# Windowed attention and a gated spatial unit on one core: every matmul operand as two float16 pieces with fixed scales

## The chip, the cores and the metric

The kernel runs on one core of one Trainium2 chip. The metric is the device time of one execution in microseconds (us); the time before is the median of three runs. One further execution was recorded by the hardware profiler, and all views below are of that one.

The engines of a core are TensorE (PE; its weight loads are listed as PEld), VectorE (DVE), ScalarE (ACT), GpSimd (POOL) and SyncE (SP), which here only issues DMAs. PE writes to PSUM. Each engine works through its instructions in the order in which the program gives them and waits on semaphores for the others.

## The reference

```python
# q, k, v: (4, 8, 768, 64) float32; window 128, 4 sink keys
scores = np.matmul(q, k.transpose(0, 1, 3, 2)) / np.sqrt(D)
keep = is_sink | in_window             # columns 0..3, or 0 <= row - column < 128
a = softmax(np.where(keep, scores, -1e9))          # (sum + 1e-9) below
x = np.matmul(a, v) -> (4, 768, 512)               # heads side by side
h = np.maximum(x @ w_in, 0.0)          # w_in (512, 1024) float64
u, v = h[..., :512], h[..., 512:]
v_n = (v - mean(v)) / np.sqrt(var(v) + 1e-06)
v_s = einsum('ts,bsd->btd', w_spatial, v_n) + b_spatial[None, :, None]
out = ((u * v_s) @ w_out).astype(np.float32)       # w_out (512, 512) float64
```

The inputs are normal draws: q and k have a spread of 0.58, v of 0.1, w_in and w_out of 0.044, w_spatial of 0.00083; b_spatial is about 1.

## The kernel before

Four batches (b), six tiles of 128 rows each (t), two halves of four heads (hf). An attention step (b, t, hf) is a block of score products (`scores`, PE L1027 or L1033, into four PSUM banks `sc`), a mask and row minimum on DVE (L1038), an exponential on ACT (L1043), a split of the weights into two float16 pieces `p high` and `p low` (`weights`), a DMA transpose (L1090), and the product with v (`attend`, L1122 to L1130). When both halves are there, `divide` (L1145 to L1150) makes x, which is split and transposed into `xT`. Then come, for each tile, the product `ps_v` with the second half of w_in, ReLU, normalisation and a split into `vn`; for each pair of tiles (c0) four products `ps_u` with the first half of w_in (d = 0..3, ring `u`), four products `ps_s` of w_spatial with all six `vn` of the batch, gate and product with u (`g`), a split into `g2`, and two products `ps_o` with w_out, whose result ACT copies and SP stores.

A split product is three matmuls: high by high, high by low, low by high (`three`, L758; `scores`, L1033; `product` in `attend`). The pieces are float16 for p, v, x, w_in, vn and w_spatial. They are fp32r (a 4-byte format; the profile writes f32) for q, k, g and w_out: `qp`, `kring`, `ksink`, `g2` and `wout`. Batch 0 has its scores in whole fp32 (L1027), and its first two tiles also the product with v (L1072 transposes, L1139), from the raw loads.

Where a float16 piece is made from v, w_in or w_spatial, it is multiplied by a power of two found at run time. For v of a batch: ACT sums |v| over each of six tiles (L908, `junk`), `all_max` takes the maximum on DVE and PE (L775 to L789: three DVE instructions, two small matmuls), `power_of_two_scale` makes the scale and its inverse (L226, L229). For w_spatial the same (L862). For each half of w_in the clamp in the decoding of float64 (`decode`, L811 on DVE) also gives the maximum, and `scale_from_high_word` makes the scale (L236 to L245). Every high piece (`high`, L726, scale read from a tile) and low piece (`low_scaled`, L747, DVE) of these, the division of the first two tiles (L1146), the ReLUs (L1189, L1237) and the gate (L1258) use such a scale. The window and sink count are compared with the values built in (`Scalars.compare`); a flag decides at the end whether a general path runs in addition.

The order of all work is computed when the kernel is built. `Plan.add` gives each piece a rank, one or more engines with a cost each, what it reads and what it writes; several engines mean that the planner picks one (`ENGINES`: `q low`, `k low`, `p low`, `vn low`, `g low` and the product with u may go to DVE or POOL; `low_scaled` is for DVE alone). Buffers come from rings of fixed size (`UB` 5 for u, `G2B` 6 for g2, `QKB` 2 for the raw q and k), most of them handed out in the order of the ranks. `PASSES` is a list of seeds with which the planner improves its order. The planner's order is then fixed, on each engine and on SP's queue of DMAs.

Of the kernel before, what the change touches and what calls it, by code (L numbers as in the profile page):

```python
# [6 lines left out]
F32 = mybir.dt.float32  # L7
# [3 lines left out]
I32 = mybir.dt.int32  # L11
# [19 lines left out]
TOP_LOW = bits_as_f32(0x39000000)  # L31
# [27 lines left out]
def f64_to_f32(nc, raw, w, tmp, top=None):  # L59

    words = raw.rearrange("p (n two) -> p n two", two=2)
    lo, hi = words[:, :, 0], words[:, :, 1]
    c = w.bitcast(I32)
    nc.scalar.activation(w, hi.bitcast(F32), AF.Abs)
    nc.scalar.activation(tmp, lo.bitcast(U32), AF.Copy, scale=2.0 ** -29)
    if top is None:
        nc.gpsimd.tensor_scalar(w, w, EXP_LOW, EXP_HIGH, op0=ALU.max, op1=ALU.min)
    else:  # L70
        nc.vector.tensor_scalar(w, w, EXP_LOW, None, op0=ALU.max, op1=ALU.max, accum_out=top)
# [147 lines left out]
SUM_SCALE, SUM_FLOOR = 2.0 ** -12, 2.0 ** -112  # L219


def power_of_two_scale(nc, pool, r, name):


    scale = pool.tile([P, 1], F32, name=name + "_scale")
    nc.vector.tensor_scalar(scale.bitcast(I32), r.bitcast(I32), 0x7F800000, 0x7F800000,  # L226
                            op0=ALU.bitwise_xor, op1=ALU.bitwise_and)
    inv = pool.tile([P, 1], F32, name=name + "_inv")
    nc.vector.reciprocal(inv, scale)  # L229
    return scale, inv  # L230


def scale_from_high_word(nc, pool, top, name):

    t = pool.tile([P, 1], F32, name=name + "_top")
    nc.vector.tensor_scalar(t, top, TOP_LOW, EXP_HIGH, op0=ALU.max, op1=ALU.min)  # L236
    n = pool.tile([P, 1], I32, name=name + "_not")
    nc.vector.tensor_scalar(n, t.bitcast(I32), 0x7FFFFFFF, 0x47F00000, op0=ALU.bitwise_xor, op1=ALU.bitwise_and)
    e = pool.tile([P, 1], I32, name=name + "_exp")
    nc.vector.tensor_scalar(e, n, 0x07FFFFFF, 3, op0=ALU.bitwise_and, op1=ALU.logical_shift_left)  # L240
    nc.vector.scalar_tensor_tensor(out=e, in0=n, scalar=0x40000000, in1=e, op0=ALU.bitwise_and, op1=ALU.bitwise_or)
    scale = pool.tile([P, 1], F32, name=name + "_scale")
    nc.vector.tensor_scalar(scale, e.bitcast(F32), 2.0 ** 12, None, op0=ALU.mult)
    inv = pool.tile([P, 1], F32, name=name + "_inv")
    nc.vector.reciprocal(inv, scale)  # L245
    return scale, inv
# [19 lines left out]
UB, VNB, G2B, XTB, P16B, PTB, QKB, QPB, PEB, VB, VRB = 5, 12, 6, 2, 2, 2, 2, 2, 2, 3, 6  # L266
# [30 lines left out]
SCALARS_AT = 27.0  # L297
COLD_TIMES, DMA_START, DMA_LAND = 2.0, 1.7, 1.5
SPELL, ENOUGH = 3.41333, 3030.0
PORT = 0.7  # L300
AHEAD, AHEAD_MOST = 0.05, 0.6
PASSES = ((1000003, 322, 354, 3), (1000006, 123, 212, 1), (1000007, 281, 383, 3), (1000008, 0, 58, 3), (1000009, 0, 11, 3), (1000014, 0, 421, 4), (1000021, 444, 0, 3), (1000329, 316, 0, 3), (1000653, 170, 138, 4), (1000927, 0, 637, 3), (1000987, 377, 68, 2), (1001045, 0, 205, 2), (1001102, 38, 0, 3), (1001131, 528, 106, 3), (1001348, 1242, 212, 4), (1001349, 404, 7, 5), (1001385, 407, 0, 4), (1001398, 113, 172, 3), (1001455, 0, 14, 2), (11000127, 339, 0, 2), (11000189, 0, 74, 3), (11000203, 522, 72, 4), (11000255, 35, 330, 2), (11000353, 0, 145, 2), (11000354, 0, 200, 2), (11000417, 37, 93, 3), (11000494, 926, 48, 2), (11000511, 687, 0, 2), (13001225, 236, 18, 2), (22000675, 339, 205, 5), (22000684, 0, 46, 2), (22000739, 49, 0, 2), (22001001, 265, 0, 2), (37000818, 27, 109, 3), (51001115, 185, 0, 3), (55001266, 648, 0, 4), (73000498, 853, 0, 3),)
# [268 lines left out]
def begin(nc, pool):  # L571
# [7 lines left out]
    st.wout = pool.tile([P, 2, KC, DM], F32R, name="wout")  # L579
# [39 lines left out]
def fast_path(tc, st, scalars, qk, v, v0, vs, w_in, w_sp, b_sp, w_out, out):  # L619
# [7 lines left out]
    with (  # L627
# [14 lines left out]
        kring = const.tile([P, 2, 4, HP, SEG], F32R, name="kring")  # L642
        ksink = const.tile([P, 2, HP, NS], F32R, name="ksink")
# [24 lines left out]
        def next_p16(name):  # L668
# [4 lines left out]
            "dec": ("u", sb([P, 1024], I32, "u", UB)), "junk": ("vr", sb([P, 1024], BF16, "vr", VB)),  # L673
            "u": ("u", sb([P, KC, TC], F32, "u", UB)), "wraw": ("u", sb([P, 1024], F32, "u", UB)),
# [6 lines left out]
            "qp": ("qp", sb([P, 2, HP, P], F32R, "qp", QPB)),  # L681
# [6 lines left out]
            "g": ("g", sb([P, TC], F32, "g", 2)),  # L688
            "g2": ("g2", sb([P, 2, TC], F32R, "g2", G2B)),
# [6 lines left out]
                 "p16": P16B, "pT": PTB, "x": 1, "x16": 2, "xT": XTB, "g": 2, "g2": G2B,  # L696
# [20 lines left out]
        def high(rank, kind, n, views, reads, writes, scale=None):  # L717

            def f(e):
                o, x = views()  # L720
                sc = scale() if scale else None
# [12 lines left out]
            plan.add(rank, ENGINES[kind], costs(kind, n, pointer=scale is not None), f, reads, writes, shared=True)  # L734
# [28 lines left out]
        vals = {}  # L763

        def begin_sums(name, n):
            m = small.tile([P, n + 1], F32, tag="mxs", name="mxs", bufs=1)
            nc.gpsimd.memset(m[:, n:], SUM_FLOOR)
            vals["mx", name] = m

        def all_max(rank, name, cols):  # L770


            def a(e):
                m = vals["m", name] = small.tile([P, 1], BF16, tag="allmax", name="allmax_m")
# [5 lines left out]
            def c(e):  # L780
                m = vals["1", name] = small.tile([1, 1], BF16, tag="allmax1", name="allmax_1")
                nc.vector.tensor_reduce(out=m, in_=tl("ps_row", name)[:1, :P], axis=AX.X, op=ALU.max)

            def d(e):
                nc.tensor.matmul(tl("ps_col", name)[:, :1], st.ones, vals["1", name], start=True, stop=True)

            def f(e):
                r = vals["r", name] = small.tile([P, 1], F32, tag="allmax2", name="allmax_r")
# [7 lines left out]
        def scalar(rank, name, f, t=0.3):  # L796
            plan.add(rank, "d", t, lambda e: f(), [("r", name)], [("scale", name)])


        def decode(rank, src, i, c, f0, top=None):  # L800
# [6 lines left out]
            def clamp(e):  # L807
                if top is None:
                    eng[e].tensor_scalar(w(), w(), EXP_LOW, EXP_HIGH, op0=ALU.max, op1=ALU.min)
                else:  # L810
                    nc.vector.tensor_scalar(w(), w(), EXP_LOW, None, op0=ALU.max, op1=ALU.max, accum_out=top())  # L811
# [578 lines left out]
```

## Time and profile before

| | before |
|---|---|
| median of three runs (lowest, highest) | 434.05 us (432.85, 434.43) |
| profiled execution | 431.45 us |
| its span, first to last instruction | 429.7 us |
| PE / PEld / DVE / ACT / POOL busy in the span | 402.0 / 310.7 / 333.8 / 280.8 / 199.5 us |
| moved by DMA | 64.57 MB |

The span is what the profile shows; 1.75 us of the profiled execution lie outside it. Busy times count an instruction from its start to its end. Matmuls overlap in the pipeline, so the length of one (some 0.27 us for 256 columns) is not its price: that is the distance from the start of one to the start of the next, or the length of a group in the chain of waits divided by its count. Idle time of an engine that is not the bottleneck costs nothing.

### The profile page before, as it was taken

What the parts mean: (1) busy time and instruction counts of PE and PEld (TensorE: products, weight loads), DVE (VectorE), ACT (ScalarE), POOL (GpSimd) and SP (SyncE); (2) the same over time, 40 slices, a digit from 0 to 9 for tenths busy, and PEclk for the clock granted to TensorE, in tenths of its full rate; (3) what the DMA queues carried; (4) which work ended last, traced back from release to release, by engine and by line L of the source; (5) the groups of instructions that cost most, each with busy time, mean ns of one, the idle gap of its engine ahead of it and who ended that gap; (6) DMA issues with size and microseconds to landing.
All of it is one profiled execution on the core that took longest, in us unless ns stands there. A gap on an engine that the chain in (4) does not pass through costs nothing.

```text
span 429.7 us, 9834 instructions
## 1 busy us (share of the span) xinstructions
PE 402.0 (94%) x3646; PEld 310.7 (72%) x3646; DVE 333.8 (78%) x924; ACT 280.8 (65%) x600; POOL 199.5 (46%) x232
## 2 busy tenths in 40 slices
PE   2779888799999999999999999999999999999994
PEld 1558356577887687778768777678777887788883
DVE  2999999998899999769989987577996786336340
ACT  3999778978986888655687675578565754231211
POOL 4425458773995746548435476306552451100000
PEclk9995689999999999999999999999999999999998
DMA  7998699982259899964764899455954355200102
GB/s 227 384 374 240 176 171 210 214 191 63 75 108 251 203 216 199 211 137 64 185 146 132 218 186 163 109 124 90 142 132 105 76 127 129 51 24 2 50 25 80
DMA packets 136039, 64.57 MB, mean 150 GB/s; under 512 B 118192, under 2 KB 122032, under 8 KB 135984
## 3 DMA queue, kind: packets, MB, share of 16 engines
q1 hardware_dynamic: 135984, 63.88, 63.3%
q8 instruction: 30, 0.49, 0.6%
q14 instruction: 25, 0.20, 0.2%
HBM read 28.73 MB, written 6.29 MB: 82 GB/s over the span
## 4 chain that ended last, share of the span: by engine, by line
PE 73%; DVE 14%; ACT 6%; issue 3%; DMA 2%; SPq 0%; POOL 0%; DVEq 0%; ACTq 0%
PE ps_s L758 20%; PE ps_o L758 15%; PE ps_u L758 12%; PE ps_v L758 12%; PE sc L1033 7%; DVE pexp L1038 2%; PE av L1128 2%; PE av L1129 2%; PE av L1130 2%; ACT pexp L1043 1%; DMA dec<-w_in 1%; DVE w L821 1%; DVE p L740 1%; DVE wsp L747 1%; DVE vring L747 1%
## 5 line engine op out<-in xcount | busy, mean ns | idle before, releaser
L758 PE MATMUL ps_s<-wsp,vn 128*128 128x256 f16 x864 | 99.0, 273 | 0.0
L1043 ACT ACTIVATE pexp<-pexp,nm 128x260 f32<-128x260 f32 (+1 forms) x192 | 82.4, 484 | 24.0 <-DVE nm L1038 22.2
L758 PEld LDWEIGHTS <-vn 128*128 128x128 f16 x864 | 82.8, 98 | 11.7 <-issue 0.8
L758 PE MATMUL ps_o<-wout,g 128*128 128x512 f32 x288 | 72.3, 402 | 0.1
L758 PE MATMUL ps_v<-win,xT 128*128 128x512 f16 x288 | 67.6, 385 | 2.6 <-ACT u L1237 2.6
L758 PE MATMUL ps_u<-xT,win 128*128 128x256 f16 x576 | 68.0, 273 | 1.2 <-ACT vr L1189 1.1
L758 PEld LDWEIGHTS <-win 128*128 128x128 f16 x576 | 55.1, 98 | 11.1 <-issue 1.8
L758 PEld LDWEIGHTS ps_o<-wout,g 128*128 128x128 f32 x288 | 52.7, 188 | 12.5 <-ACT ob L1284 0.3
L740 DVE TENSOR_TENSOR p<-pexp,p 128x16 f16<-128x16 f32 (+2 forms) x65 | 56.2, 881 | 4.5 <-ACT p L724 3.9
L758 PEld LDWEIGHTS <-xT 128*128 128x128 f16 x288 | 27.2, 99 | 34.8 <-issue 5.0
L1205 POOL TENSOR_TENSOR rs<-rs,mhalf 128x1 f32<-128x1 f32 x24 | 17.1, 714 | 55.2 <-DVE rs L1199 55.2
L724 ACT CAST p<-pexp 128x32 f16<-128x32 f32 (+2 forms) x69 | 41.8, 627 | 1.1 <-DMA pT<-p 0.6
L740 POOL TENSOR_TENSOR x<-x,x 128x512 f16<-128x512 f32 x24 | 31.6, 1316 | 21.3 <-ACT x L724 20.9
L1258 DVE SCALAR_TENSOR_TENSOR g<-ps_s,isc,b_bc 128x256 f32<-128x256 f32 x48 | 23.0, 480 | 21.1 <-PE ps_s L758 20.0
L724 ACT CAST g<-g 128x256 fp32r<-128x256 f32 x35 | 14.1, 404 | 35.1 <-DVE g L1262 25.6
L1128 PE MATMUL av<-vring,pT 128*128 128x65 f16 x328 | 35.4, 195 | 1.5 <-DMA pT<-p 1.5
L1033 PE MATMUL sc<-kring,qp 64*128 64x260 f32 (+1 forms) x432 | 36.2, 297 | 0.5 <-DVE nm L1038 0.5
L1033 PEld LDWEIGHTS sc<-kring,qp 64*128 64x128 f32 x432 | 28.6, 186 | 9.5 <-issue 6.5
L1130 PE MATMUL av<-vring,pT 128*128 128x65 f16 x328 | 35.3, 195 | 0.0
L1129 PE MATMUL av<-vring,pT 128*128 128x65 f16 x328 | 35.3, 195 | 0.0
L1128 PEld LDWEIGHTS <-pT 128*128 128x128 f16 x328 | 30.8, 99 | 2.7 <-DMA pT<-p 1.7
L1237 ACT ACTIVATE u<-ps_u,icu 128x256 f32<-128x256 f32 x48 | 22.6, 470 | 13.7 <-PE ps_u L758 13.2
(142 smaller groups left out, 741.0 us busy)
## 6 DMA issues: line engine op xcount, KB each, us to landing
qkraw<-qk_t SPq DMA_DIRECT2D x18, 512.0 KB, 4.5
out<-ob SPq DMA_DIRECT2D x24, 256.0 KB, 2.5
vraw<-v_s SPq DMA_DIRECT2D x22, 256.0 KB, 4.2
dec<-w_in SPq DMA_DIRECT2D x8, 512.0 KB, 6.7
dec<-w_out SPq DMA_DIRECT2D x4, 512.0 KB, 6.6
wsp<-qk_t SPq DMA_DIRECT2D x6, 256.0 KB, 6.3
qkraw<-qk_t SPq DMA_DIRECT2D x6, 256.0 KB, 4.8
pT<-p SPq DMA_TRANSPOSE x88, 2.9
```

The source lines that it names most:

```text
L724: nc.scalar.copy(o, x)
L740: eng[e].tensor_tensor(out=o, in0=x, in1=hi, op=ALU.subtract)
L747: nc.vector.scalar_tensor_tensor(out=o, in0=x, scalar=scale(), in1=hi, op0=ALU.mult, op1=ALU.subtract)
L758: nc.tensor.matmul(o, a, m, start=(i == 0), stop=(i == n - 1))
L1033: nc.tensor.matmul(o, qp[rows, qi, hp, :], keys(kring[:, ki], rows), start=(m == 0), stop=(m == 2))
L1043: nc.scalar.activation(po, po, AF.Exp, bias=nm()[:, h2 + q:h2 + q + 1], scale=-1.0)
L1128: nc.tensor.matmul(o[:, h], ph, vh, start=(t < 2 and j == 0), stop=False)
L1129: nc.tensor.matmul(o[:, h], ph, vl, start=False, stop=False)
L1130: nc.tensor.matmul(o[:, h], pl, vh, start=False, stop=(j == nb - 1 and (t < 2 or h == HH - 1)))
L1205: nc.gpsimd.tensor_tensor(out=vals["rs", i], in0=vals["rs", i], in1=mhalf, op=ALU.pow)
L1237: plan.add(r + WHEN["u relu"], "a", 0.36, lambda e: nc.scalar.activation(tl("u", (b, c0))[:, d, :], tl("ps_u", i)[:, :TC], AF.Relu, scale= ...
L1258: nc.vector.scalar_tensor_tensor(out=g(), in0=tl("ps_s", i)[:, :TC], scalar=vals["s", "sp"][1], in1=b_bc[:, t0:t0 + TC], op0=ALU.mult, op1 ...
```

## The change

The scales become constants (16 for q and k, 128 for v, w_in, w_out and for u, 16384 for w_spatial), and with them q, k, g and w_out become pairs of float16 too. So `begin_sums`, `scalar`, `v_scale`, `scale_half`, `power_of_two_scale` and `scale_from_high_word` go; `high` and `low_scaled` take a number. `q low` and `k low` change from `low` (DVE or POOL) to `low_scaled` (DVE), and so does the low piece of w_out (POOL before).

In place of the scales there are range checks at the end of the work: ACT sums |x| of v, of q and k, of w_in and w_out pieces, and of the rows of w_spatial, which are loaded once more (`measure`); the ReLU of u gives its sum as well; `checks` joins them into the flag that decides on the general path. For the inputs above each sum lies well inside its limits. The rank of the new pieces is late (`CHECKS_AT` 56; two steps after the tile's for q and k, four for v).

The ring of u grows from 5 to 7 buffers, that of g2 from 6 to 12 (of half the size). Some costs in the planner are new, and `PASSES` has other seeds, so the whole order is computed anew.

```diff
-UB, VNB, G2B, XTB, P16B, PTB, QKB, QPB, PEB, VB, VRB = 5, 12, 6, 2, 2, 2, 2, 2, 2, 3, 6
+UB, VNB, G2B, XTB, P16B, PTB, QKB, QPB, PEB, VB, VRB = 7, 12, 12, 2, 2, 2, 2, 2, 2, 3, 6
...
-    st.wout = pool.tile([P, 2, KC, DM], F32R, name="wout")
+    st.wout = pool.tile([P, 2, KC, DM], F16, name="wout")
...
-        kring = const.tile([P, 2, 4, HP, SEG], F32R, name="kring")
-        ksink = const.tile([P, 2, HP, NS], F32R, name="ksink")
+        kring = const.tile([P, 2, 4, HP, SEG], F16, name="kring")
+        ksink = const.tile([P, 2, HP, NS], F16, name="ksink")
...
-            "qp": ("qp", sb([P, 2, HP, P], F32R, "qp", QPB)),
+            "qp": ("qp", sb([P, 2, HP, P], F16, "qp", QPB)),
...
-            "g2": ("g2", sb([P, 2, TC], F32R, "g2", G2B)),
+            "g2": ("g2", sb([P, 2, TC], F16, "g2", G2B)),
...
+        def measure(rank, kind, i, n, x, reads, scale):
+            def f(e):
...
+                nc.scalar.activation(o, a, AF.Abs, scale=scale, accum_out=sums[:, first[kind] + i:first[kind] + i + 1])
+            plan.add(rank, "a", 0.22 + n / 1200, f, reads, [("sum", kind, i)])
...
             def clamp(e):
-                if top is None:
-                    eng[e].tensor_scalar(w(), w(), EXP_LOW, EXP_HIGH, op0=ALU.max, op1=ALU.min)
-                else:
-                    nc.vector.tensor_scalar(w(), w(), EXP_LOW, None, op0=ALU.max, op1=ALU.max, accum_out=top())
+                eng[e].tensor_scalar(w(), w(), EXP_LOW, EXP_HIGH, op0=ALU.max, op1=ALU.min)
...
-            all_max(r, name, lambda: mx)
-            scalar(r, name, lambda: vals.__setitem__(
-                ("s", name), scale_from_high_word(nc, scal, vals["r", name], f"win{half}")), 1.0)
...
+            for k in range(2):
+                measure(CHECKS_AT, "win", 2 * half + k, 1024, lambda k=k: win[:, 0, 2 * k:2 * k + 2, f0:f0 + 512],
+                        [("win", half)], 1.0 / F16_RANGE)
...
+                load(CHECKS_AT, "wrow", c, lambda c=c: w_rows[c * P:(c + 1) * P, :], 384, lambda t: t[:, :S])
+                measure(CHECKS_AT, "wsp", c, S, lambda c=c: tl("wrow", c)[:, :S], [("wrow", c)], SP_SCALE / F16_RANGE)
...
-                plan.add(r0 + gap * c, "a", 0.52, lambda e, c=c, i=i: nc.scalar.copy(wout[:, 0, c, :], tl("w32", i)),
-                         [("w32", i)], [("wout", c, 0)])
-                low(r0 + gap * c, "w_out low", 512, lambda c=c, i=i: (wout[:, 1, c, :], tl("w32", i), wout[:, 0, c, :]),
-                    [("w32", i), ("wout", c, 0)], [("wout", c, 1)])
+                high(r0 + gap * c, "w_in high", 512, lambda c=c, i=i: (wout[:, 0, c, :], tl("w32", i)),
+                     [("w32", i)], [("wout", c, 0)], OUT_SCALE)
+                low_scaled(r0 + gap * c, 512, lambda c=c, i=i: (wout[:, 1, c, :], tl("w32", i), wout[:, 0, c, :]), OUT_SCALE,
+                           [("w32", i), ("wout", c, 0)], [("wout", c, 1)])
...
+        def checks():
...
+            plan.add(CHECKS_AT, "d", 0.2, bound, [("sum", "wsp"), ("b_col", 0)], [("mx", "gate")])
+            all_max(CHECKS_AT, "gate", lambda: vals["mx", "gate"])
...
+            plan.add(CHECKS_AT, "d", 0.5, early, [("sum", k) for k in ("v", "win", "wout", "wsp", "qk")], [("most", 0)])
+            plan.add(CHECKS_AT, "d", 0.4, late, [("sum", "u"), ("r", "gate"), ("most", 0)], [("marks", 0)])
+            plan.add(CHECKS_AT, "PE", 0.06, count, [("marks", 0)], [("ps_row", "marks")], columns=26)
+            plan.add(CHECKS_AT, "d", 0.6, decide, [("ps_row", "marks"), ("flag", 0)], [("decision", 0)])
...
+            measure(r + 2, "qk", (b - WHOLE) * NT + t, 1024, lambda: raw().rearrange("p c h s -> p (c h s)"), [("qkraw", i)], Q_SCALE / F16_RANGE)
-            low(r, "q low", 512, lambda: (qp()[:, 1], raw()[:, 0], qp()[:, 0]), [("qkraw", i), ("qp", i, 0)], [("qp", i, 1)])
+            low_scaled(r, 512, lambda: (qp()[:, 1], raw()[:, 0], qp()[:, 0]), Q_SCALE, [("qkraw", i), ("qp", i, 0)], [("qp", i, 1)])
...
-            plan.add(r + WHEN["div"], "d", 1.05, divide, [("av", (b, t))] + ([("scale", ("v", b))] if whole_av(b, t) else []), [("x", (b, t))])
+            plan.add(r + WHEN["div"], "d", 1.05, divide, [("av", (b, t))], [("x", (b, t))])
...
-            plan.add(r + WHEN["u relu"], "a", 0.36, lambda e: nc.scalar.activation(
-                tl("u", (b, c0))[:, d, :], tl("ps_u", i)[:, :TC], AF.Relu, scale=vals["icu", b]),
...
+            plan.add(r + WHEN["u relu"], "a", 0.55, lambda e: nc.scalar.activation(
+                tl("u", (b, c0))[:, d, :], tl("ps_u", i)[:, :TC], AF.Relu, scale=G_SCALE / (V_SCALE * IN_SCALE),
+                accum_out=sums[:, k:k + 1]), [("ps_u", i)], [("u", (b, c0), d), ("sum", "u", k)])
...
+                measure(r + 4, "v", b * NT + t, DM, v_raw(b, t)[1], [v_raw(b, t)[0]], V_SCALE / F16_RANGE)
```

## Rows read from the trace of the kernel before

**Rows 1.** The page, parts 1 and 2: busy times, and granted clock in 40 slices.

```profile
PE 402.0 (94%) x3646; PEld 310.7 (72%) x3646; DVE 333.8 (78%) x924; ACT 280.8 (65%) x600; POOL 199.5 (46%) x232
...
PEclk9995689999999999999999999999999999999998
```

**Rows 2.** Windows: stretch, its length, busy time (instructions) of each engine, clock, DMA.

```profile
20.00:60.00 40.00, 34.96 (x191) 23.60 (x189) 38.17 (x125) 35.42 (x77) 18.84 (x20) 0.74 0.91 251
60.00:100.00 40.00, 34.64 (x356) 24.68 (x357) 38.46 (x97) 33.91 (x70) 29.20 (x25) 0.96 0.84 186
100.00:260.00 160.00, 159.28 (x1606) 125.38 (x1604) 142.75 (x375) 119.24 (x265) 95.10 (x96) 1.00 0.74 162
260.00:424.00 164.00, 163.74 (x1456) 129.58 (x1454) 102.24 (x285) 78.98 (x164) 47.67 (x55) 1.00 0.42 90
```

**Rows 3.** Waits of PE: who waited for whom, us in total, times, longest.

```profile
PE sc L1027 <- DMA qkraw<-qk_t: 4.8, 1, 4.8
PE tr L1072 <- DVE nm L1038: 4.0, 2, 2.0
```

**Rows 4.** The chain of waits near the end: start us, us, what.

```profile
344.60 0.93 PE sc L1033 x12
...
375.50 2.60 PE ps_v L758 x12
...
383.35 11.79 PE ps_s L758 x108
395.14 5.59 PE ps_o L758 x24
...
423.82 0.59 ACT ob L1284
```

**Rows 5.** Timeline of PE from 84 us: start us, us, then the instructions.

```profile
84.48 0.88 PE L1033 MATMUL sc<-kring,qp 64*128 64x128 f32 x12
85.30 0.28 PE L1122 MATMUL av<-vsink,pT 96*128 96x260 f16 x1
...
85.75 0.19 PE L1130 MATMUL av<-vring,pT 128*128 128x65 f16 x1
85.78 0.20 PE L1128 MATMUL av<-vring,pT 128*128 128x65 f16 x1
```

**Rows 6.** Timeline of PE in the first 60 us.

```profile
21.32 1.97 PE L1139 MATMUL av<-vring,pT 128*128 128x65 f32 x8
...
42.98 2.10 PE L1027 MATMUL sc<-wsp,qkraw 64*128 64x260 f32 x8
45.01 4.22 PE L758 MATMUL ps_v<-win,xT 128*128 128x512 f16 x12
...
58.32 1.15 PE L1027 MATMUL sc<-wsp,qkraw 64*128 64x260 f32 x8
```

**Rows 7.** Timeline of DVE at 32 us.

```profile
32.13 0.17 DVE L229 RECIPROCAL v_inv<-v_scale 128x1 f32<-128x1 f32 x1
```

**Rows 8.** Groups by line and form: count, busy us, mean ns, idle before.

```profile
L740 POOL TENSOR_TENSOR kring<-qkraw,kring 128x512 fp32r<-128x512 f32 x11 | 16.1, 1463 | 0.3
L740 POOL TENSOR_TENSOR qp<-qkraw,qp 128x512 fp32r<-128x512 f32 x11 | 14.7, 1336 | 5.9 <-ACT qp L724 5.9
...
L747 DVE SCALAR_TENSOR_TENSOR vring<-vraw,v_scale,vring 128x512 f16<-128x512 f32 x22 | 19.7, 897 | 1.5 <-ACT vring L726 1.5
L811 DVE TENSOR_SCALAR_CACHE_REDUCE w<-w 128x512 f32<-128x512 f32 x8 | 5.4, 676 | 2.2 <-ACT w L813 2.2
...
L724 ACT CAST p<-pexp 128x1024 f16<-128x1024 f32 x32 | 33.3, 1040 | 1.0 <-DMA pT<-p 0.6
L1237 ACT ACTIVATE u<-ps_u,icu 128x256 f32<-128x256 f32 x48 | 22.6, 470 | 13.7 <-PE ps_u L758 13.2
L726 ACT ACTIVATE vring<-vraw,v_scale 128x512 f16<-128x512 f32 x22 | 15.7, 717 | 0.0
L908 ACT ACTIVATION_READ_ACCUMULATOR junk<-vraw 128x1 f32 x22 | 4.2, 189 | 0.0
```

More of the change, by code (lines that the diff above doesn't have):

```diff
@@ L56, in compare, with f64_to_f32 @@
         v.tensor_copy(self.flagi, self.flag)
-def f64_to_f32(nc, raw, w, tmp, top=None):
+def f64_to_f32(nc, raw, w, tmp):
     words = raw.rearrange("p (n two) -> p n two", two=2)
@@ L216, in general_path @@
                 nc.sync.dma_start(out[b, t * P:(t + 1) * P, :], o)
[L219 to L246, printed above, removed]
+Q_SCALE, V_SCALE, IN_SCALE, OUT_SCALE, SP_SCALE, G_SCALE = 2.0 ** 4, 2.0 ** 7, 2.0 ** 7, 2.0 ** 7, 2.0 ** 14, 2.0 ** 7
+F16_RANGE = 2.0 ** 16
+LEAST, MOST = 2.0 ** -6, 0.99
+VN_MOST = DM ** 0.5
 NS = 4
@@ L608, in begin @@
     nc.vector.tensor_copy(st.ident16, st.ident)
-    st.ones = pool.tile([1, P], BF16, name="ones")
+    st.ones = pool.tile([P, P], BF16, name="ones")
     nc.vector.memset(st.ones, 1.0)
+    st.b_col = pool.tile([P, NT], F32, name="b_col")
     mhalf = pool.tile([P, 1], F32, name="mhalf")
@@ L616, in begin, with fast_path @@
     return st
-def fast_path(tc, st, scalars, qk, v, v0, vs, w_in, w_sp, b_sp, w_out, out):
+def fast_path(tc, st, scalars, qk, v, v0, vs, w_in, w_sp, w_rows, b_sp, b_col, w_out, out):
     nc = tc.nc
@@ L720, in f @@
                 o, x = views()
-                sc = scale() if scale else None
+                sc = scale
                 if e == "a":
@@ L733, in f @@
                     nc.gpsimd.tensor_scalar(o, x, 1.0 if sc is None else sc, 1.0, op0=ALU.mult, op1=ALU.mult)
-            plan.add(rank, ENGINES[kind], costs(kind, n, pointer=scale is not None), f, reads, writes, shared=True)
+            plan.add(rank, ENGINES[kind], costs(kind, n), f, reads, writes, shared=True)
         def low(rank, kind, n, views, reads, writes):
@@ L780, in c @@
             def c(e):
-                m = vals["1", name] = small.tile([1, 1], BF16, tag="allmax1", name="allmax_1")
+                m = vals["1", name] = small.tile([1, 1], BF16, tag="allmax1", name="allmax_1", bufs=1)
                 nc.vector.tensor_reduce(out=m, in_=tl("ps_row", name)[:1, :P], axis=AX.X, op=ALU.max)
             def d(e):
-                nc.tensor.matmul(tl("ps_col", name)[:, :1], st.ones, vals["1", name], start=True, stop=True)
+                nc.tensor.matmul(tl("ps_col", name)[:, :1], st.ones[:1], vals["1", name], start=True, stop=True)
             def f(e):
-                r = vals["r", name] = small.tile([P, 1], F32, tag="allmax2", name="allmax_r")
+                r = vals["r", name] = small.tile([P, 1], F32, tag="allmax2", name="allmax_r", bufs=1)
                 nc.vector.tensor_copy(r, tl("ps_col", name)[:, :1])
@@ L914, in v_scale, with sink_values @@
+        def sink_values(b, r):
             for hf in range(2):
@@ L951, in value @@
         def value(b, t, r):
-            name, sl = ("v", b), (b * NT + t) % NV
+            sl = (b * NT + t) % NV
             key, raw = v_raw(b, t)
+            if not whole_av(b, t):
+                load(early.get(("v", t), r - 1) if b == 0 else r - 1, "vraw", (b, t), lambda: v[b, t * P:(t + 1) * P, :], 256)
             if sl not in seen_slots:
@@ L1282, in o_piece @@
             r0 = TC * c0 + k * P
-            plan.add(r, "PE", 2.83, product, [("g2", (b, c0, d)) for d in range(KC)] + [("wout", c) for c in range(KC)], [("ps_o", i)], columns=6144)
-            plan.add(r + WHEN["o copy"], "a", 0.5, lambda e: nc.scalar.copy(tl("ob", i), tl("ps_o", i)), [("ps_o", i)], [("ob", i)])
+            plan.add(r, "PE", 2.62, product, [("g2", (b, c0, d)) for d in range(KC)] + [("wout", c) for c in range(KC)], [("ps_o", i)], columns=6144)
+            plan.add(r + WHEN["o copy"], "a", 0.5, lambda e: nc.scalar.activation(tl("ob", i), tl("ps_o", i), AF.Copy, scale=1.0 / (G_SCALE * OUT_SCALE)), [("ps_o", i)], [("ob", i)])
             plan.add(r + WHEN["o store"], "SP", 0.37, lambda e: nc.sync.dma_start(out[b, r0:r0 + P, :], tl("ob", i)),
@@ L1332, in fast_path, with tile_kernel @@
                 f(e)
-def tile_kernel(tc, qk, v, v0, vs, n_sink, window, w_in, w_sp, b_sp, w_out, out):
+def tile_kernel(tc, qk, v, v0, vs, n_sink, window, w_in, w_sp, w_rows, b_sp, b_col, w_out, out):
     nc = tc.nc
```

193 lines of the change are left out of this document (94 added, 99 removed).

## The prediction

> **What bounds the kernel now.** I read the busy times and the clock line first [rows 1]: PE is busy 402.0 of 429.7 us, 94%, far ahead of DVE with 78%, and its granted clock is full except in the fourth to sixth slices. But an average mixes stages, so the windows come next [rows 2]. They show two kernels. From 100 to 424 us PE is busy 159.28 of 160 and 163.74 of 164 us at clock 1.00: there nothing but PE's own work sets the time, and a microsecond taken from it is a microsecond of the end. From 20 to 100 us DVE is the fullest (38.17 and 38.46 of 40 us), ACT is close behind (35.42 and 33.91), and PE, with 34.96 of 40, works at granted clock 0.74, so that its busy time is inflated. The waits of PE [rows 3] are few and all of the start: on the first load, then on DVE's row minima. The chain's end [rows 4] is PE alone: the last `ps_o`, then 0.59 us of ACT and the store. So the change has to be priced twice: by PE's work after about 84 us, and by what delays the start.
>
> **PE's work.** Prices are group lengths divided by counts, not the lengths of single matmuls. Twelve float16 matmuls of `ps_v` with 512 columns take 2.60 us; 24 of `ps_o` with fp32r weights and the same columns take 5.59, 2.80 for twelve [rows 4]. As float16 `ps_o` should cost what `ps_v` does: 24 groups x 0.20 = 4.8 us.
>
> The score blocks are 36 (batches 1 to 3, twelve each); 30 have 260 columns, six (t = 0) have 128. A block of 260 columns takes 0.93 us [rows 4], 0.155 for each pair of matmuls on the two row halves. `ps_s` prices float16 at 11.79 / 108 = 0.109 us for 256 columns [rows 4], so 0.111 for 260; a block should take 6 x 0.111 = 0.67, if a pair streams together as it does now. That saves 0.26 x 30 = 7.8 us. A t = 0 block runs from 84.48 to 85.30, 0.82 us [rows 5]; by columns it would be 6 x 0.055 = 0.33. I keep 0.07 for the switch into the row halves and take 0.40: 0.42 x 6 = 2.5 us. That float16 weights load unseen even behind very short matmuls is shown by `av`: with other weights each time and 65 columns, the next starts 0.03 us later (85.75 to 85.78) [rows 5]. The sum on PE is 15.1 us. Its bounds: 4.8 if score blocks gain nothing, 16 if the 0.07 goes too; the loss is with the rivals.
>
> Most of the fourteen small matmuls of the scale searches go; at a few hundredths each I count nothing.
>
> **The start.** The product with v of the first tile was issued up to 21.32 us and ran 1.97 [rows 6], until 23.29; its division waits for the inverse scale of v, which starts at 32.13 and takes 0.17 [rows 7]. From there the tile goes through split and transpose to the first `ps_v` at 45.01 [rows 6]. With a constant scale 32.30 - 23.29 = 9.0 us of that path have no cause left. Similarly the pieces of w_in, of v and later of w_spatial need no search. But DVE is full here, so a shorter path helps only as far as DVE loses work: the clamps with maximum are 5.4 us [rows 8], and I estimate another 6 from some 35 tiny instructions of the searches at the 0.17 us of the one shown [rows 7]. Against that stand plain clamps (I put half on POOL and take 2 us back), and four low pieces of w_out at up to 0.90 each, 3.6 us, by the nearest row, `vring` [rows 8]. Net 6 us by load, 9.0 by path; ACT is also relieved, as its sums over v and w_spatial move away. I take 8. Bounds: nothing, if the new order fills the gap with other loads, up to 18 (rival B).
>
> **What is added, and its cover.** ACT gets 18 sums over raw q and k and six over weights, of 1,024 elements. The nearest row is the cast of 1,024 at 1.04 us, plus up to 0.19 for reading the accumulator [rows 8]: 25 to 30 us. The 48 ReLUs of u get that read as well, up to 9.1 us; their scale is no longer read from a tile, which may give part back (between zero and a tenth each; I take zero). ACT grows by 34 to 39, to at most 320 of some 410 us. It has 85 us free from 260 to 424 and 41 from 100 to 260 [rows 2], and PE's backlog covers it. A sum over q and k holds one of two raw buffers; the load that wants the buffer stands in SP's queue, and behind it the transposes of p, for which `av` waits. Now PE has `ps_u`, `ps_s` and `ps_o` to run meanwhile; without that each such wait costs up to 1.2 us, 22 in all.
>
> DVE gets the low pieces of q and k that POOL had: eleven and eleven [rows 8], at 0.90 by `vring` 19.7 us, with w_out 23; it loses about 9. From 100 to 260 us DVE has 17 us free [rows 2], and PE's savings shrink the window by some 8. So something must move to POOL, which is rid of 16.1 + 14.7 us [rows 8] and may take `p low`, `g low` and products with u. That fits, though tightly: I give back 2 us, between 0 and 13 (rival D).
>
> The check at the end needs the last sums of u, far ahead of the last `ps_s` and `ps_o`, and rows of w_spatial that wait for buffers of the u ring. Its three small matmuls stand in PE's order; if a sum is late, PE waits. I count nothing; the other end is one late sum of 1.2 us and half a dozen short steps, about 3 us. The 2.4 MB more of loads fall where DMA has room (share 0.42 after 260 us) [rows 2]. Longer rings remove no PE work; they let it be at hand, and are part of that cover.
>
> **Sum.** The profiled execution is 431.45 us: 431.45 - 15.1 - 8 + 2 = 410.4. It lay 2.6 below the median of the runs shown, so the time to expect is 413.
>
> **Rival B, the start clears altogether.** At 0.74 in 20 to 60 us, half of that stretch was at the low level (1.2 of 2.4 GHz) [rows 2]: the same eight score matmuls take 2.10 us at 42.98 and 1.15 at 58.32 [rows 6]. If `ps_v` arrives 10 us sooner and PE has no gaps, the clock stays up sooner; half of 20 us, 10, comes on top: 403. For it: full clock goes with a full PE from 100 on [rows 2]. Against: DVE stays full in the stretch. The Trainium skill, "TensorE: Matmul & The Clock Gate", Part 1, says that the throttled state is the default and sustained activity releases it; the rows agree.
>
> **Rival C, only part of it does what it says.** The score blocks gain nothing, since the pair is held by something other than the format: 431.45 - 4.8 - 8 + 2 = 420.7, so 423. Against: the extra of `ps_o` over `ps_v`, 0.017 us for each weight load, explains most of the distance from 0.67 to 0.93.
>
> **Rival C', the halves stop overlapping.** If float16 pairs ran one after the other, a block would take 12 x 0.111 = 1.33 us, 0.40 more than now: +12 on 30 blocks, -1 on the six short ones. With the other terms 431.45 + 11 - 4.8 - 8 + 2 = 431.7, so 434: no change. Against: 0.93 for twelve now is 0.078 each, below the 0.111 of one alone. The same page's section "Back-to-back issue gap" speaks for it: it gives some 81 ns at 128 columns as the sustained price of a weight load with its matmul. By it twelve would take 0.97 us, more than the 0.82 of now; the 0.03 us of `av` contradicts it.
>
> **Rival D, slower: DVE sets the time until 260 us.** If the net 12 to 14 us on DVE aren't moved off, at its present share in 20 to 260 us (219.4 of 240) that is 14 us more, PE's gain before 260 turns into idle time, and about half of the 15.1 remains after it: 431.45 + 14 - 7.5 = 438, so 440. The start's gain is used up in that. It decides where DVE is over 97% in 100 to 260 us and PE idles over 5 there. For it: 142.75 of 160 now. Against: POOL's 95.10 of 160, and freedom in who does what.
>
> **Chances.** The forecast has 0.58 (its own range 405 to 421), B 0.16, C 0.12, C' 0.04, D 0.10, about one in ten of D within 0.5% of before. A change under 0.5% can't be told from none. Faster 0.86, same 0.05, slower 0.09. The range takes in the forecast, C and most of B: 400 to 427.
>
> **What would show it.** `ps_o` groups of 2.60; score blocks of about 0.67, short ones near 0.40; the first `ps_v` at 35 to 38 us; PE over 98% from 90 us to its end, DVE below 97% in 100 to 260; the same 6 us after PE's last matmul. The prediction is wrong if score blocks stay at 0.9, if PE idles after 100 us, or if the first `ps_v` is still beyond 43.

## The result and the profile after

The changed kernel takes 417.18 us (median of four runs, 416.74 to 418.16) against 433.45 us (432.60 to 434.43) for the kernel before: ratio 0.963, 95% interval 0.960 to 0.966. It is faster by 16 us; the forecast was 413, the range 400 to 427. Its profiled execution took 416.92 us with a span of 415.1 us, 14.6 us less than the span before. All of the accounting below is between these two spans; the medians differ by 1.7 us more, which is not divided.

Part 1 of the page, as in [rows 1]:

```profile
PE 389.8 (94%) x3635; PEld 274.7 (66%) x3635; DVE 325.7 (78%) x908; ACT 299.3 (72%) x695; POOL 164.9 (40%) x204
```

PE's busy time fell by 12.2 us, ACT's rose by 18.5, POOL's fell by 34.6. The windows of the same stretches as in [rows 2] (the last one now ends where PE's work does):

```profile
20.00:60.00 40.00, 36.18 (x221) 25.20 (x221) 38.95 (x104) 33.01 (x70) 17.11 (x20) 0.96 1.11 265
60.00:100.00 40.00, 36.78 (x406) 25.16 (x405) 39.23 (x104) 35.64 (x86) 22.62 (x24) 0.96 0.95 175
100.00:260.00 160.00, 158.38 (x1651) 112.14 (x1649) 142.99 (x398) 127.15 (x300) 81.50 (x90) 1.00 0.75 165
260.00:409.00 149.00, 146.84 (x1315) 103.78 (x1313) 92.30 (x259) 89.42 (x214) 35.34 (x37) 1.00 0.50 112
```

The picture is that of before: from 100 us on PE is nearly full (158.38 of 160; 159.28 before), and until then DVE is, now more so (38.95 and 39.23 of 40). The waits of PE, as in [rows 3], are again of the start, with xT late once, and have one at the end, behind the last product:

```profile
PE sc L1011 <- DMA qkraw<-qk_t: 5.3, 2, 4.8
PE ps_v L732 <- DMA xT<-x: 3.2, 1, 3.2
...
PE ps_row L887 <- DVE marks L884: 0.9, 1, 0.9
```

The chain of waits, against [rows 4]; groups of score products first, then its end:

```profile
155.79 0.77 PE sc L1017 x12
...
163.59 0.44 PE sc L1017 x12
...
395.89 5.18 PE ps_o L732 x24
...
401.59 5.34 PE ps_o L732 x24
406.93 0.12 PE ps_col L772
...
408.92 0.14 DVE flagi L898
```

Read here: a block of 260 columns takes 0.77 us, a short one 0.44, 24 matmuls of `ps_o` 5.18. After the last `ps_o` the chain no longer goes through ACT's `ob` to the store; it goes through a dozen short steps of the range check, 406.93 to 409.06, and the program ends 6.0 us after the flag is written. The gap between PE's last product and the end of the span grew from 5.9 to 8.2 us.

The start, against [rows 6], on PE, and the first x on DVE:

```profile
37.69 2.40 PE L1011 MATMUL sc<-wsp,qkraw 64*128 64x260 f32 x8 [0.27 <-issue]
40.02 4.25 PE L732 MATMUL ps_v<-win,xT 128*128 128x512 f16 x12
44.20 1.15 PE L1011 MATMUL sc<-wsp,qkraw 64*128 64x260 f32 x8
```

```profile
23.27 0.69 DVE L1134 TENSOR_TENSOR x<-av,den 128x512 f32<-128x512 f32 x1
```

The first x is divided 9.7 us earlier than before (the path of [rows 7] is gone), but the first `ps_v` comes only 5.0 us earlier. Before, the division stood here:

```profile
32.98 0.69 DVE L1150 TENSOR_TENSOR x<-av,den 128x512 f32<-128x512 f32 x1
```

With these rows the 14.6 us divide into: `ps_o` 24 groups x (5.59 - 5.18) / 2 = 4.9; score blocks 30 x 0.16 = 4.8 and 6 x 0.38 = 2.3; the end -2.3; and the start 4.9, which is what remains. The work that is left at 100 us agrees: PE then has 21 matmuls of `ps_u`, 48 of `av` and 24 of scores fewer still to do than it had before the change; at 0.109, 0.03 and 0.064 us each that is some 5 us.

### The profile page after: what moved, and what is told of

It is laid out like the page before. It is cut to its first block, busy times and chain, and to the rows that moved or that the text cites. A ratio compares the mean times of both kernels' runs of the same rounds, so it can differ in the third digit from the quotient of the medians.

```text
span 415.1 us, 9851 instructions
## 1 busy us (share of the span) xinstructions
PE 389.8 (94%) x3635; PEld 274.7 (66%) x3635; DVE 325.7 (78%) x908; ACT 299.3 (72%) x695; POOL 164.9 (40%) x204
## 4 chain that ended last, share of the span: by engine, by line
PE 63%; DVE 26%; ACT 4%; issue 3%; DMA 3%; SPq 0%; DVEq 0%; ACTq 0%
PE ps_s L732 19%; PE ps_o L732 14%; PE ps_u L732 11%; PE ps_v L732 9%; DVE pexp L1022 5%; DVE p L714 5%; PE sc L1017 5%; ACT pexp L1027 2%; PE av L1112 2%; DMA dec<-w_in 2%; PE av L1113 2%; PE av L1114 2%; DVE vring L721 1%; DVE w L791 1%; DVE wsp L721 1%
## 5 line engine op out<-in xcount | busy, mean ns | idle before, releaser
L732 PE MATMUL ps_u<-xT,win 128*128 128x256 f16 x576 | 69.7, 275 | 2.8 <-ACT vr L1173 1.9
L732 PE MATMUL ps_o<-wout,g 128*128 128x512 f16 x288 | 65.3, 379 | 1.2 <-DVE g L1243 0.4
L714 DVE TENSOR_TENSOR p<-pexp,p 128x16 f16<-128x16 f32 (+2 forms) x65 | 50.0, 783 | 7.5 <-ACT p L698 6.3
L732 PEld LDWEIGHTS <-g 128*128 128x128 f16 x288 | 27.5, 98 | 32.6 <-issue 2.2
L698 ACT CAST p<-pexp 128x1024 f16<-128x1024 f32 (+2 forms) x68 | 40.6, 621 | 1.3 <-DMA pT<-p 0.7
L1243 DVE SCALAR_TENSOR_TENSOR g<-ps_s,b_bc 128x256 f32<-128x256 f32 x48 | 20.2, 422 | 19.1 <-PE ps_s L732 18.6
L1112 PE MATMUL av<-vring,pT 128*128 128x65 f16 x328 | 34.1, 193 | 0.0
L1114 PE MATMUL av<-vring,pT 128*128 128x65 f16 x328 | 34.0, 193 | 0.0
L1113 PE MATMUL av<-vring,pT 128*128 128x65 f16 x328 | 34.0, 193 | 0.0
L1112 PEld LDWEIGHTS <-pT 128*128 128x128 f16 x328 | 30.2, 97 | 1.5 <-issue 0.6
L1113 PEld LDWEIGHTS <-pT 128*128 128x128 f16 x328 | 30.1, 97 | 0.6
L1222 ACT ACTIVATE u<-ps_u 128x256 f32<-128x256 f32 x48 | 18.2, 379 | 16.6 <-PE ps_u L732 16.4
L1114 PEld LDWEIGHTS <-pT 128*128 128x128 f16 x328 | 30.0, 97 | 0.0
L698 ACT CAST g<-g 128x256 f16<-128x256 f32 x36 | 14.5, 403 | 20.4 <-DVE g L1247 18.2
```

The lines of the kernel that those rows point to most:

```text
L698: nc.scalar.copy(o, x)
L714: eng[e].tensor_tensor(out=o, in0=x, in1=hi, op=ALU.subtract)
L732: nc.tensor.matmul(o, a, m, start=(i == 0), stop=(i == n - 1))
L1112: nc.tensor.matmul(o[:, h], ph, vh, start=(t < 2 and j == 0), stop=False)
L1113: nc.tensor.matmul(o[:, h], ph, vl, start=False, stop=False)
L1114: nc.tensor.matmul(o[:, h], pl, vh, start=False, stop=(j == nb - 1 and (t < 2 or h == HH - 1)))
```

## Experiments

In every experiment but two, the order of the work was held fixed: pieces were emptied, narrowed or moved in the finished order, so that the planner did not make another order. The two are the old seeds and the matmuls alone. Ratios are to the kernel before on the same chip, with 95% intervals. The first three groups divide the change, the fourth prices a score block (one execution), the last asks what bounds the start.

### The change in two halves

Three kernels were made from the kernel before, in its order: with float16 formats alone, with constant scales alone (searches and their sums emptied), and with both. None has a range check.

```diff
-    st.wout = pool.tile([P, 2, KC, DM], F32R, name="wout")
+    st.wout = pool.tile([P, 2, KC, DM], F16, name="wout")
...
-        kring = const.tile([P, 2, 4, HP, SEG], F32R, name="kring")
+        kring = const.tile([P, 2, 4, HP, SEG], F16, name="kring")
```

```diff
-            m = scal.tile([P, NT + 1], F32, name=f"mxv{b}")
-            vals["mx", name] = m
...
+            vals["s", name] = 2.0 ** 7, 2.0 ** -7
+            vals["icv", b] = vals["icu", b] = 2.0 ** -14
```

Formats alone, expected:

> The kernel before in its own order with one part of the change: q, k, g and w_out as float16 pairs; scales searched at run time as before (q, k, g and w_out unscaled). Theory: PE does 12 us less after 84 us (24 groups of 0.21, 30 score blocks of 0.16, six of 0.37), and PE alone sets that stretch: 421 to 422. Rival: DVE and ACT can't follow at that pace from 100 to 260 us, and under 8 us come through: 426 or more.

Constants alone, expected:

> The kernel before in its own order with the other part: constant scales, so that the searches (sums over v and w_spatial, maxima, scales, inverse scales) are left out; formats, engines and buffers as before. Theory: DVE's load sets the start, it falls by some 9 us before 100 us, but the order is fixed and PE at its low clock follows: 4 to 6 us less, 428 to 429.5. Rival by path: the division of the first tile is 9 us sooner and all of it reaches the end: 424 to 425. Third: loads set the start, and nothing changes: 433.

Both, expected:

> The kernel before in its own order with both parts, formats and constants, and no range check. Theory: the two parts add up, 12 plus 5, 416 to 417; as the changed kernel carries 2.3 us for its check, the new order, longer rings and engines then were worth little. Rival: the new order and the longer rings were needed for the gain: 421 or more.

Measured: formats alone 422.88 us, ratio 0.974 (0.970 to 0.978), 11.1 us less; constants alone 427.98, 0.987 (0.983 to 0.991), 6.0 less; both 416.95, 0.960 (0.956 to 0.964), 17.1 less. The two parts add up without loss, and the rivals fell. The formats give nearly the 12.0 us that the rows of PE add up to. The constants give 6.0, by the interval 4 to 7, which takes in the 4.9 of the start.

They do not give it by the path of the first x. With constants alone, in the order of before, that x is divided only 1.4 us earlier, and the first `ps_v` starts 1.5 us earlier:

```profile
31.55 0.69 DVE L1153 TENSOR_TENSOR x<-av,den 128x512 f32<-128x512 f32 x1
```

```profile
43.54 3.98 PE L758 MATMUL ps_v<-win,xT 128*128 128x512 f16 x12
```

So neither the 9.7 us of the first x nor the 5.0 us of the first `ps_v` in the changed kernel measures what the start is worth.

### The old seeds

The changed kernel with `PASSES` of the kernel before, so that the planner makes another order from the same pieces.

> The changed kernel with the seeds of the kernel before for the planner's order, all else as changed. Theory: the order matters only in the first 100 us, PE is full afterwards in any good order: within 4 us of the changed kernel, 417 to 421. Rival: much of the 16 us is the search for the order: 425 or more.

Measured: 428.56 us, ratio 0.988 (0.984 to 0.992). The theory that the order matters little fell: with this order, which was not searched for these pieces, 11 of the 16 us are gone. The windows of the first 100 us show where most of them went:

```profile
20.00:60.00 40.00, 28.61 (x172) 20.77 (x172) 39.53 (x98) 36.70 (x81) 14.87 (x17) 0.82 1.05 271
60.00:100.00 40.00, 35.18 (x396) 24.48 (x394) 39.38 (x107) 36.99 (x86) 20.73 (x22) 0.97 0.98 194
```

DVE is as full as in the changed kernel, but with other things first: in 20 to 60 us it finishes 23 row minima of scores instead of 28, and PE is busy 28.61 us instead of 36.18. The halves above kept the order of before and lost nothing; this new set of pieces needed a search of its own. What the searched order is worth beyond that cannot be told here: the changed kernel without its check, in the next group, has ratio 0.957 (0.954 to 0.960), and both halves in the order of before have 0.960 (0.956 to 0.964).

### The range check and the sums

First the check itself was left out (the steps that join the sums into the flag), then the sums as well, with the second load of w_spatial. In the third, complete kernel the steps of the check stand earlier in the fixed order: the maximum before the last `ps_u`, the count before the last two groups of `ps_o`.

```diff
             def early(e):
+                return
...
             def count(e):
+                return
```

```diff
+        moved = [chain[x] for x in ("b", "c", "d", "f", "late", "count", "decide")]
...
+        order = [x for x in order if x[0] not in moved]
...
+        put(last_u, "b")
...
+        put(o[2], "count")
+        put(o[2] + 1, "decide")
```

> The changed kernel in its own order with the last pieces of the range check left out (maximum over the gate, counting, decision); all sums stay. Theory: the end waits for the flag, which is written 2.1 us after PE's last real matmul, and the span's last stretch falls from 8.2 to about 5.9 us; with the 0.4 us that PE waits for the check, 2.3 to 2.7 us less, 414.5. Rival: the 6 us after the last matmul are the store of the last tile and the branch, whatever the flag does: no change, 417.

> As the run without the check, and all sums of the range check left out as well (18 over q and k, six over weights, 24 over v, six over rows of w_spatial with their loads, and the accumulation in the ReLU of u), 40 us or so of ACT's 299. Theory: PE's backlog hides them, so under 1.5 us less than without the check, 413 to 414.5. Rival: ACT holds up the attention steps between 60 and 260 us and its relief comes through: 4 us or more less, 410 or below.

> The changed kernel complete, with the pieces of the check put earlier in the fixed order: its matmuls before the last product of u, before the fourth to last and before the second to last product with w_out, and into the banks of the scores, which are free by then. Theory: the decision is there about 5 us before PE ends, so the same 2.3 to 2.7 us are saved as without the check: 414.5 and the fastest complete version. Rival: moving the pieces makes PE wait elsewhere, or the tail is not the check's: 417.

The changed kernel itself, run beside them, took 417.42 us, ratio 0.965 (0.962 to 0.968). Without the check: 414.63, 0.957 (0.954 to 0.960). Without the sums too: 415.76, 0.960 (0.958 to 0.963), so the sums cost nothing that can be measured, although ACT's busy time falls from 299.0 to 250.5 us with them. Decided earlier: 414.92, 0.958 (0.956 to 0.961), 2.5 us better than the changed kernel, with everything computed. Its PE at the end:

```profile
397.18 5.35 PE L732 MATMUL ps_o<-wout,g 128*128 128x512 f16 x24
402.46 0.17 PE L888 MATMUL tr<-marks,ones 128*1 128x26 bf16 x1
402.57 5.35 PE L732 MATMUL ps_o<-wout,g 128*128 128x512 f16 x24
```

The count stands between two `ps_o` groups and waits for nothing; the span ends 5.8 us after PE again (407.9 to 413.7). So the check's price was its place, 2.3 to 2.8 us, not its work.

### Matmuls alone: what a score block costs

A kernel of matmuls without the rest of the computation: blocks of 12 or 24 products on alternating row halves (the upper or the lower 64 of the 128 rows; 260 columns, as a score block), each followed by 18 or 36 products on all rows (256 columns), in float16 and in fp32r; and six products of 260 columns on all rows in place of a block.

```diff
+        for _ in range(20):
+            halves16(12)
+            full256(18)
+        for _ in range(10):
+            halves16(24)
+            full256(36)
```

> A kernel of matmuls alone, from one tile of q (nothing of the reference is computed). First a cold PE with 96 whole fp32 matmuls on row halves, 48 of 512 columns in float16, and both again. Then 20 times (12 row-half matmuls of 260 columns in float16, 18 of 256 on all rows), ten times (24, 36), the same two with fp32r row halves, 20 times (6 of 260 on all rows, 18), and 48 of 512 columns in fp32r and float16. Theory: what a score block costs beyond 6 x 0.111 us is one change between row halves and all rows, 0.10 us: the stage of ten is 1.0 us shorter than that of twenty in float16, and the stage without row halves is 2.0 us shorter. With fp32r each pair costs 0.15, so the float16 stage of twenty is 3 to 3.5 us shorter. Rival: a pair of row halves costs 0.128 in float16 itself, and ten are as long as twenty. On the clock: whole fp32 matmuls leave it low however full PE is, so both stages of 96 start at 0.26 per matmul or fall back to it; rival: a full PE raises it whatever it computes, and the second stage of 96 runs at 0.13.

The timeline of PE (start, length, instruction), first float16, then fp32r, then without row halves:

```profile
69.66 0.84 PE L36 MATMUL bank<-xf 64*128 64x260 f16 x12
70.43 2.14 PE L51 MATMUL bank<-xf 128*128 128x256 f16 x18
72.50 0.84 PE L36 MATMUL bank<-xf 64*128 64x260 f16 x12
...
126.50 1.50 PE L36 MATMUL bank<-xf 64*128 64x260 f16 x24
127.94 4.10 PE L51 MATMUL bank<-xf 128*128 128x256 f16 x36
131.97 1.50 PE L36 MATMUL bank<-xf 64*128 64x260 f16 x24
...
181.23 0.99 PE L41 MATMUL bank<-xf32r 64*128 64x260 f32 x12
182.15 2.14 PE L51 MATMUL bank<-xf 128*128 128x256 f16 x18
...
240.90 1.69 PE L41 MATMUL bank<-xf32r 64*128 64x260 f32 x24
242.53 4.10 PE L51 MATMUL bank<-xf 128*128 128x256 f16 x36
...
297.41 0.83 PE L46 MATMUL bank<-xf 128*128 128x260 f16 x6
...
300.04 0.83 PE L46 MATMUL bank<-xf 128*128 128x260 f16 x6
```

Taken from start to start, a float16 block of 12 lasts 70.43 - 69.66 = 0.77 us, one of 24 lasts 1.44: twelve more cost 0.67, and 0.10 is paid once. In fp32r it is 0.92 and 1.63: twelve more cost 0.71, and 0.21 is paid once. So the forecast's 0.111 for a pair is right, but fp32r pairs are nearly as cheap (0.118, where 0.15 was expected); what float16 takes away is mostly a fixed 0.11 per block. The group on all rows pays too: 18 products last 2.07 and 36 last 4.03, so 1.96 for 18 and 0.11 once. The starts of the single instructions in the trace show where: the pairs of a float16 block stand 0.107 us apart, but the group behind starts 0.204 after the last pair, and the next block 0.205 after the last product of that group, whose own step is 0.109. In fp32r it is the first pair of a block that takes 0.222. One round without row halves, which changes its banks as well, lasts 300.04 - 297.41 = 2.63, against 2.84 with them: 0.21 for leaving and returning, twice what was expected. The Trainium skill, "TensorEngine Tiling (Array Packing)", section "Key Properties", says that changing the tiling mode drains the engine, without a figure; here it is 0.10 us each way.

The theory on the clock fell too. The first stage of whole fp32 products lasts 23.67 us, the second 21.31, or 0.111 for each of the 192 steps that the profile lists, with a clock of 1.00 recorded in both: whole fp32 products did not keep a full PE at the low level.

### What bounds the start

Three experiments on DVE's load before 100 us. In the first, DVE computes nine low pieces of p twice; in the second, two in-place steps of decoding w_in and w_out are left out, so the weights are others, the check sends the work to the general path afterwards, and the run is read up to the flag; in the third, on top of the earlier decision, four of the nine low pieces go to POOL.

```diff
+                    done.append(1)
+                    if len(done) <= 9:
+                        eng[e].tensor_tensor(out=o, in0=x, in1=hi, op=ALU.subtract)
```

```diff
             def clamp(e):
+                return
```

```diff
+        for k in PLOWS:
+            order[lows[k]] = order[lows[k]][0], "p"
```

> The changed kernel; DVE computes the nine low pieces of p of 1,024 columns that it has before 100 us twice over, the second time with the same result. They take 1.34 us each in the trace of the changed kernel, so DVE gets 12.1 us more work in a stretch (20 to 100 us) where it is busy 78.18 of 80 us. Theory (by load): until about 100 us the start is as long as the work of DVE, whatever path is shorter; the end moves by 9 to 12 us, to 426 to 430 (ratio 0.983 to 0.992), and PE's loss before 100 us grows by as much. Rival (by path): the start hangs on the chain of the first tiles and on the low clock of PE; the second copies lie behind what others wait for and fill waits of DVE; the end moves by under 3 us, to 420 at most (ratio under 0.970).

> The changed kernel without two of the steps of decoding w_in and w_out, the clamp and the masking of the exponent (so the weights are not the reference's). Both work in place, so nothing else changes. In the trace of the changed kernel they are 5 x 0.77 and 6 x 0.65 us of DVE in 20 to 100 us, 7.8 us together, and some more before 20 us. Theory (by load): the end comes 6 to 9 us earlier, 409 to 412 (ratio 0.943 to 0.951). Rival (by path): the weights are in place before the first product with them waits for its tile, so under 2 us are gained, 415.5 to 417.5 (ratio over 0.958).

> The complete changed kernel with the earlier decision, and four of the nine low pieces of p of 1,024 columns before 100 us given from DVE to POOL, at places where POOL idles (about 42, 48, 61 and 94 us); the order stays. DVE loses 4 x 1.22 = 4.9 us. Theory (by load): the end comes 3 to 5 us earlier than with the earlier decision alone (ratio 0.9584), 410 to 412 (0.947 to 0.952). Rival: a low piece takes 2.2 us on POOL, and small DVE instructions beside one took 2.0 us where 0.17 is usual, so that DVE gets nothing back, or the piece's later end holds the transposes of p; 414 to 417 (0.956 to 0.963).

More on DVE: 429.19 us, ratio 0.990 (0.987 to 0.994), 11 to 12 us for 12.1 us of work: one to one, as the theory by load has it. But the run does not separate load from path. Its rival took the second copies (here L718) to lie behind what others wait for, and they do not: on DVE each stands ahead of a small low piece of the same step, and the chain of waits goes through it.

```profile
78.67 2.03 DVE p L714
80.72 2.96 DVE p L718
```

Less on DVE: the flag is written at 407.63 us, against 408.92 in the profile of the changed kernel and 409.42 in a second one, so 1.3 to 1.8 us for 7.8 us of work. That is what the rival has; the theory by load asked for 6 to 9. First this run, then the second profile:

```profile
407.63 0.14 DVE L898 CAST flagi<-found_any 1x1 int32<-1x1 f32 x1
```

```profile
409.42 0.14 DVE L898 CAST flagi<-found_any 1x1 int32<-1x1 f32 x1
```

The windows of the run with less on DVE:

```profile
20.00:60.00 40.00, 32.08 (x215) 21.14 (x215) 36.11 (x95) 34.36 (x73) 17.76 (x20) 0.79 1.12 265
60.00:100.00 40.00, 36.80 (x413) 25.45 (x411) 38.01 (x102) 36.22 (x86) 20.92 (x25) 0.96 1.04 182
```

DVE now has 5.9 us free of 80, where the changed kernel has 1.8. The longest pieces of its chain in 20 to 100 us are transfers (two more of them left out here) and a product at half rate:

```profile
13.64 8.83 DMA dec<-w_in
39.31 4.68 PE ps_v L732 x12
...
67.44 5.58 DMA qkraw<-qk_t
```

So the load of DVE alone does not set the start: with 7.8 us of it gone, other waits take its place after 1.3 to 1.8 us, and in the chain these are transfers and PE's own rate. How load and path share the 11 to 12 us of the first run stays open.

Lows on POOL: 417.67 us, ratio 0.964 (0.960 to 0.968); with the earlier decision alone it was 0.958, so nothing is gained and probably 2 us lost (the intervals still touch). The groups of DVE in 20 to 100 us, first of the kernel with the earlier decision, then with the four pieces on POOL:

```profile
L714 DVE TENSOR_TENSOR p<-pexp,p 128x1024 f16<-128x1024 f32 x9 | 12.1, 1339 | 0.5 <-ACT p L698 0.3
...
L721 DVE SCALAR_TENSOR_TENSOR vring<-vraw,vring 128x512 f16<-128x512 f32 x6 | 5.3, 884 | 0.0
...
L714 DVE TENSOR_TENSOR p<-pexp,p 128x16 f16<-128x16 f32 x8 | 4.5, 568 | 0.0
```

```profile
L715 DVE TENSOR_TENSOR p<-pexp,p 128x16 f16<-128x16 f32 x8 | 8.3, 1032 | 0.4 <-ACT p L699 0.4
L715 DVE TENSOR_TENSOR p<-pexp,p 128x1024 f16<-128x1024 f32 x5 | 7.2, 1439 | 0.2
L724 DVE SCALAR_TENSOR_TENSOR vring<-vraw,vring 128x512 f16<-128x512 f32 x6 | 7.2, 1196 | 0.0
```

DVE is rid of 4.9 us of large pieces, but eight tiny ones grow from 4.5 to 8.3 us and six of `vring` from 5.3 to 7.2: 5.7 us come back, and its windows stay full (38.84 and 39.32 of 40). As DVE did not get emptier, the run says nothing on what a smaller load would bring. The Trainium skill, "SBUF — State Buffer", section "Who interferes with whom", says that a DVE instruction with two inputs in SBUF contends with a POOL instruction that reads SBUF; the trace agrees: the longest of these six `vring` pieces, 2.56 us at 95.59, runs beside a low piece of p on POOL, and the shortest take 0.68.

## Why the prediction came out as it did

The direction and the range were right, and so was the mechanism on PE; how the start gains is not settled. The median was 4.2 us above the forecast. From profile to profile the miss is 416.92 - 410.4 = 6.5 us: the forecast also carried over the 2.6 us by which the profile of before lay under its median, and after the change that distance is 0.3, so 2.3 us of the miss were hidden by luck. Step by step:

- **`ps_o`**: 4.8 forecast, 4.9 measured.
- **Score blocks of 260 columns**: 7.8 forecast, 4.8 measured; the largest error of the PE part. The step that failed is "a block should take 6 x 0.111 = 0.67". It divided a whole block by its pairs and so took 0.155 for a price per pair. A block is pairs and a fixed part: 6 x 0.118 + 0.21 in fp32r, 6 x 0.111 + 0.10 in float16. The remaining 0.10 x 30 is the missing 3.0 us. The forecast had kept 0.07 for the switch in the short blocks, and forgot it in the long ones. **Short blocks**: 2.5 and 2.3. (The upper bound of the PE sum is 15.1 + 6 x 0.07 = 15.5, not 16.)
- **Start**: 8 forecast, 4.9 measured by the trace, 6.0 by the constants alone. By path, the first x came 9.7 us earlier, as the 9.0 had it, but that is not what reached the end: with constants alone it came 1.4 earlier, and the gain was no smaller. By load 6 was too much: in the same stretch DVE has nine low pieces of p of 1,024 columns (12.1 us) where there were five (6.1), and six low pieces of q and k where there were two. In part that is work of later steps, which now fall into the stretch (52 row minima where there were 44). Taking 8, between load and path, was the error. Which of DVE's load, the transfers and PE's own rate sets the 5 us is not shown; the run with less on DVE says only that its load was not the last limit.
- **Give-back after 100 us**: 2 forecast; PE idles 1.6 us from 100 to 260 us where it idled 0.7 before, so at most 0.9. DVE is at 142.99 of 160 us, as before, and POOL has even less to do (81.50 for 95.10). Rival D asked for DVE over 97% and 5 us of idle PE, and fell by its own condition.
- **Check at the end**: 0 forecast, other end 3; measured 2.3 by the trace, 2.8 and 2.5 by the runs. The sums were in time, as forecast. What was not counted is that the planner may place the check's short steps behind the last product, where nothing covers them. That the 2 us given back and these 2.3 nearly cancel in the sum is luck.
- **Sums on ACT**: no time forecast, none measured. ACT's busy time grew by 18.5 us where 34 to 39 were forecast. The ReLU of u lost 91 ns with its scale as a constant and got 194 for the sum, where the forecast had taken zero and 189:

```profile
L1222 ACT ACTIVATE u<-ps_u 128x256 f32<-128x256 f32 x48 | 18.2, 379 | 16.6 <-PE ps_u L732 16.4
L1222 ACT ACTIVATION_READ_ACCUMULATOR u<-ps_u 128x1 f32 x48 | 9.3, 194 | 0.0
```

The terms come to 12.0 + 4.9 - 2.3 = 14.6 against 15.1 + 8 - 2 = 21.1. Rival B's condition did come, in part: eight score products at full rate (1.15 us) stand at 44.20 us, where [rows 6] has them at 58.32. It was not worth the rival's 10 us: the whole start gained 4.9, and PE had little to run, busy 2.13 of the 5 us from 45 on. How much of the 4.9 us came from it is not separated. Rivals C and C' are excluded by the 0.77 of a block. What the forecast left out altogether is the order: it let the planner fit the pieces at 2 us, and the same pieces in an order not searched for them cost 11 more than in the searched one.

## What to carry to other kernels

Divide a group into a fixed part and a price per instruction before scaling it: time it at two lengths, or read the steps inside it, above all where the array changes its mode. Work that only has to be done at some time before the end wants a place of its own ahead of the last long products; left to a rank it may land behind them. Work added to a full engine and work taken from it need not have the same price: here 12.1 us more cost 11 to 12, and 7.8 us less gave 1.3 to 1.8, as other waits stood close behind. And work moved to another engine is saved only if the pieces that stay do not get longer; time them before and after the move.

## What was not expected of the hardware

- Leaving row halves for all rows and coming back costs 0.10 us each way at full rate (steps of 0.204 and 0.205 us where 0.107 and 0.109 are usual); an fp32r block pays 0.11 more on its first pair (0.222).
- The granted clock as the profile records it can miss its low level. From 30 to 40 us the profile after has 1.00, the second profile of the same kernel 0.50 (the lower of the two levels, 1.2 GHz), and PE does the same in both; in the profile after, eight score products take 2.40 us at 37.69 and 1.15 at 44.20. The lengths of like groups decide. The window in each profile, after first:

```profile
30.00:40.00 10.00, 9.38 (x35) 6.78 (x33) 9.79 (x20) 7.17 (x16) 2.92 (x2) 1.00 1.11 235
```

```profile
30.00:40.00 10.00, 9.38 (x36) 6.76 (x35) 9.80 (x21) 7.17 (x16) 2.93 (x2) 0.50 1.12 284
```

  The profile of before has it too: its record is 1.00 from 25 to 30 us, where eight score products take 2.11 us as they do later at 0.50. So the 0.74 of [rows 2], from which rival B took half of 20 to 60 us to be at the low level, understates the low stretch: groups of eight still take 2.02 us at 51.29.

```profile
25.04 2.11 PE L1027 MATMUL sc<-wsp,qkraw 64*128 64x260 f32 x8
```

```profile
25.00:30.00 5.00, 2.97 (x15) 1.85 (x16) 4.83 (x20) 4.39 (x13) 1.27 (x1) 1.00 1.09 358
```

- An ACT instruction on 128x256 went from 470 to 379 ns when its scale became a constant (382 with constants alone, without the sum). The Trainium skill, "ScalarE: Activation LUTs", section "What ACT_TABLE_LOAD costs", gives some 93 ns for each such operand; the trace agrees with 91.
